# First four chunks of a gated recurrence taken whole instead of in halves, in a kernel that also runs an MLP

## The chip, the cores and the metric

The kernel runs on one core of a Trainium2 chip. The metric is the device time of one execution in microseconds (us). The engines are TensorE (PE, the matrix unit), VectorE (DVE), ScalarE (ACT), GpSimd (POOL) and SyncE (SP, which issues the DMAs here). Each engine works through its own list of instructions in order and waits on semaphores for the others.

## The reference

A gated linear recurrence over 768 steps, for 4 batches of 8 heads with 48 channels, feeds a two-layer MLP with a Mish-like gate.

```
f = 1 / (1 + exp(-f_logit))
for t in range(S):
    state = f[t] * state + outer(k[t], v[t])      # per batch and head, 48 x 48
    y[t] = q[t] @ state
x = y as (3072 tokens, 384)
h = x @ w_in                                       # (3072, 2048)
g = h * tanh(log1p(exp(h)))
out = g @ w_out                                    # (3072, 384)
```

## The kernel before

**The recurrence.** It is cut into 24 chunks of 128 steps: chunks 0 to 3 are the first of the four batches, chunks 4 to 7 the second of each, and so on. A chunk holds 4 pairs of heads (`NP`), a head on 64 rows each. `load` fetches the chunk's gate logits (`l`), keys and queries (`kq`) and values (`v`). `prep` forms the running sum of the log gates (on PE with a triangular matrix for chunks 0 to 3, by a scan on DVE later), then multiplies keys by its exponential (`inv`, on POOL for chunks 1 to 7) and queries by the inverse (on DVE, L373). `attn0` multiplies keys by queries (the scores), DVE masks them to the causal part into `a`. `attn1` transposes the keys on PE and ACT copies them to `kt`. `attn2` multiplies keys by values (the update). `attn3` forms the outputs `y`, and `leave` rounds them on ACT (L751, the high part of `xt`), subtracts that on PE with the matrix `minus` (L754) and copies the rest on ACT (L756, the low part). A small DMA then moves some rows of `xt` (L763).

Before the change a chunk is worked in two halves of 64 steps (`CH`). Scores are 64x64 blocks within a half. The update of the first half gives `mid`, the state between the halves, copied by ACT for chunks 0 to 3 (L648); that of the second half added to it gives `tmp` (DVE, L655), and POOL multiplies it by the chunk's decay into `state` (L740). The outputs sum products of queries with `mid` (and with `state`, from chunk 4 on) and of values with the masked scores (L673, L686). Chunk 3 (`ALONE`) has 18 further products (`pads`, L712), with weights in two small tiles lent by `g` and `n`, that place the fourth pair's rows where the other chunks use the DMA.

**The MLP.** Tokens come in 6 groups of 512, the four chunks of a batch position each (`GC` = 4). A unit is a group and one of the 16 slices of 128 hidden columns. Its first product `moe_in` (L297, 9 matmuls into `h`) needs `xt` of all four chunks, so the first one needs chunks 0 to 3 done. `mish` follows (ACT L311 exp, DVE L312, ACT L308, L314 and L315, DVE L316 for `g`, ACT L317 for `gh`, DVE or POOL for `gl`), then the second product `moe_out` (L324, 9 matmuls into `o`). `h` has two buffers, so the third unit's first product waits for `g` of the first unit. The weights of a slice arrive packed (`raw`, 768 KB, two buffers) and are split into a high and a low part by `split_w`: ACT L429, DVE L431, L432 and L434, ACT L436 (`wh`), DVE L437 (`wl`). The buffer is free when DVE L434 has read it.

**The order.** All of this is a list of steps, and the table `ORDER` gives the place of each step in its engine's list; a cost table in class `Plan` predicts when each starts. The loop in `issue` puts products on a tile of zeros (`idle`, L417) into PE's list ahead of the first second product wherever the plan has a gap:

```
while at + 527.0 < self.start[i]:
    self.idle()
    at += 427.0 if at > 6500.0 else 853.0
```

Of the kernel before, what the change touches and what calls it, by code (L numbers as in the profile page):

```python
# [159 lines left out]
class Plan:  # L160
# [61 lines left out]
    def issue(self):  # L222
        at = self.FREE["pe"]
        for i in self.order():
            engine, cost, issue = self.steps[i][:3]
            if engine == "pe":

                if self.start[i] <= self.start[self.until]:
                    while at + 527.0 < self.start[i]:
                        self.idle()  # L230
                        at += 427.0 if at > 6500.0 else 853.0
# [23 lines left out]
def recurrence_moe_kernel(  # L255
# [73 lines left out]
    with tc.tile_pool(name="work", bufs=1) as pool, tc.tile_pool(  # L329
# [327 lines left out]
        def attn3(n):  # L657
# [57 lines left out]
            def outputs():  # L715
# [5 lines left out]
                if n == ALONE:  # L721
                    pads()
# [310 lines left out]
```

## Time and profile before

| | us |
|---|---|
| median of 3 runs | 484.88 (484.2 to 486.53) |
| profiled execution, time | 487.03 |
| profiled execution, span from first to last instruction | 485.2 |
| PE busy in the span | 472.3 (97%) |
| ACT busy | 389.5 (80%) |
| DVE busy | 301.9 (62%) |
| POOL busy | 133.5 (28%) |

The span is what the profile's views divide. The profiled execution took 487.03 us, 1.8 us more than its span and 2.2 us more than the median. A busy PE is not a PE at its peak: its clock and the overlap of small products are read separately.

### The profile page before, as it was taken

The page shows a single profiled execution, that of the slowest core. Times are in us where ns is not written, and L with a number is a line of the kernel's source. Part 1 is how long each engine was busy: PE and PEld are TensorE (multiplying, and loading weights), DVE is VectorE, ACT ScalarE, POOL GpSimd, SP SyncE. Part 2 cuts the span into 40 slices and gives each one's busy share as a digit, 9 for nine tenths or more (in the row PEclk, how much of TensorE's full clock was granted, in tenths as well). Part 3 has the DMA queues.
Part 4 walks back from the last instruction along what each step waited for, and adds up shares of the span by engine and source line. Part 5 has one row for each costly group of instructions (what it writes and reads, how often), then busy time and mean ns, then how long its engine had stood idle before and what let it go on. Part 6 is the DMA issues. An engine that isn't in the chain of part 4 may idle for free.

```text
span 485.2 us, 11761 instructions
## 1 busy us (share of the span) xinstructions
PE 472.3 (97%) x4810; PEld 386.9 (80%) x4810; DVE 301.9 (62%) x523; ACT 389.5 (80%) x722; POOL 133.5 (28%) x125
## 2 busy tenths in 40 slices
PE   8898999999999999999999999999999999999995
PEld 6675778888888888888888888888888888888884
DVE  5886999999967766756557555655745433432221
ACT  6988899999996877987877887896776686867671
POOL 4522101000333124232423223243223242332422
PEclk9998999999999999999999999999999999999999
DMA  8975284365532582263435033253262000100001
GB/s 299 398 223 179 104 296 117 142 202 184 183 128 64 153 266 64 73 180 87 136 92 177 1 99 88 75 156 92 84 164 68 22 12 0 38 30 1 0 0 70
DMA packets 56604, 57.57 MB, mean 119 GB/s; under 512 B 36320, under 2 KB 39776, under 8 KB 56544
## 3 DMA queue, kind: packets, MB, share of 16 engines
q1 hardware_dynamic: 56544, 56.77, 37.8%
q8 instruction: 38, 0.62, 0.5%
q14 instruction: 22, 0.18, 0.1%
HBM read 43.25 MB, written 10.49 MB: 111 GB/s over the span
## 4 chain that ended last, share of the span: by engine, by line
PE 92%; DMA 3%; ACT 2%; issue 1%; DVE 1%; SPq 0%; ACTq 0%
PE o L324 41%; PE h L297 40%; DMA raw<-ww 3%; PE at L686 3%; PE at L602 3%; PE at L673 2%; PE at L536 2%; PE at L568 0%; PE at L754 0%; PE o L417 0%; ACT wt L429 0%; DVE wt L432 0%; DVE wt L434 0%; ACT xt L751 0%; PE at L486 0%
## 5 line engine op out<-in xcount | busy, mean ns | idle before, releaser
L319 POOL TENSOR_TENSOR gl<-g,gh 128x512 fp32r<-128x512 f32 x80 | 105.5, 1323 | 283.8 <-ACT gh L317 267.3
L297 PE MATMUL h<-xt,wh 128*128 128x512 f32 x576 | 180.6, 395 | 0.0
L297 PEld LDWEIGHTS h<-xt,wh 128*128 128x128 f32 x576 | 107.1, 189 | 23.0 <-DVE g L316 0.3
L316 DVE SCALAR_TENSOR_TENSOR g<-n,half,h 128x512 f32<-128x512 f32 x96 | 71.5, 745 | 82.6 <-ACT n L315 65.4
L324 PE MATMUL o<-gh,wh 128*128 128x512 f32 x288 | 113.4, 394 | 0.0
L297 PE MATMUL h<-xt,wl 128*128 128x512 f32 x288 | 112.9, 392 | 0.0
L324 PE MATMUL o<-gh,wl 128*128 128x512 f32 x288 | 112.2, 390 | 0.0
L324 PE MATMUL o<-gl,wh 128*128 128x512 f32 x288 | 112.2, 390 | 0.0
L311 ACT ACTIVATE n<-h 128x512 f32<-128x512 f32 x96 | 56.9, 592 | 42.5 <-PE h L297 41.9
L312 DVE TENSOR_SCALAR n<-n 128x512 f32<-128x512 f32 x96 | 42.6, 444 | 53.2 <-ACT n L311 52.8
L308 ACT ACTIVATE n<-n 128x512 f32<-128x512 f32 x96 | 60.1, 627 | 15.1 <-DVE n L312 14.8
L314 ACT ACTIVATE n<-n,ones 128x512 f32<-128x512 f32 x96 | 69.1, 720 | 1.7
L317 ACT ACTIVATE gh<-g 128x512 fp32r<-128x512 f32 x96 | 59.7, 623 | 7.1 <-DVE g L316 6.8
L297 PEld LDWEIGHTS h<-xt,wl 128*128 128x128 f32 x288 | 54.4, 189 | 11.5
L324 PEld LDWEIGHTS o<-gh,wh 128*128 128x128 f32 x288 | 54.1, 188 | 11.6
L324 PEld LDWEIGHTS o<-gl,wh 128*128 128x128 f32 x288 | 54.1, 188 | 11.3
L324 PEld LDWEIGHTS o<-gh,wl 128*128 128x128 f32 x288 | 54.1, 188 | 10.8
L315 ACT ACTIVATE n<-n 128x512 f32<-128x512 f32 x96 | 60.3, 628 | 1.6
L491 DVE TENSOR_TENSOR_SCAN cum<-go,l 128x512 f32<-128x512 f32 x20 | 27.8, 1392 | 2.8 <-ACT l L482 1.3
L373 DVE TENSOR_TENSOR kq<-kq,at 128x512 f32<-128x512 f32 (+1 forms) x38 | 25.3, 669 | 5.7 <-ACT at L499 3.8
L758 DVE TENSOR_TENSOR xt<-at,xt 128x256 fp32r<-128x256 f32 x32 | 13.0, 420 | 15.3 <-ACT xt L751 14.7
L602 PE MATMUL at<-v,kt 64*64 64x48 f32 x672 | 20.5, 221 | 1.8 <-issue 1.7
(135 smaller groups left out, 477.5 us busy)
## 6 DMA issues: line engine op xcount, KB each, us to landing
raw<-ww SPq DMA_DIRECT2D x16, 768.0 KB, 5.2
kq<-kq SPq DMA_DIRECT2D x23, 512.0 KB, 4.5
v<-vn SPq DMA_DIRECT2D x23, 256.0 KB, 4.5
l<-fl SPq DMA_DIRECT2D x20, 256.0 KB, 4.1
out<-ob SPq DMA_DIRECT2D x18, 256.0 KB, 3.0
kd<-inv SPq DMA_DIRECT2D x64, 64.0 KB, 2.2
kt<-kd SPq DMA_DIRECT2D x16, 256.0 KB, 2.9
xt<-xt SPq DMA_DIRECT2D x23, 128.0 KB, 2.7
```

The source lines that it names most:

```text
L297: nc.tensor.matmul(h, w[:, j, a * P : (a + 1) * P], xt[:, :, a, x, :], start=(n == 0), stop=(n == 3 * NK - 1))
L308: ("act", T_ACT(GT), 0, lambda: nc.scalar.activation(n, n, AF.Square))
L311: ("act", T_ACT(GT, True), 0, lambda: nc.scalar.activation(n, h, AF.Exp)),
L312: ("dve", 70 + GT / 1.92, 1, lambda: nc.vector.tensor_scalar(n, n, U_CAP, 1.0, ALU.min, ALU.add)),
L314: ("act", T_ACT(GT, False, 1), 0, lambda: nc.scalar.activation(n, n, AF.Ln, bias=ones)),
L315: ("act", T_ACT(GT), 0, lambda: nc.scalar.activation(n, n, AF.Exp, scale=-1.0)),
L316: ("dve", 662, 0, lambda: nc.vector.scalar_tensor_tensor(g, n, half_, h, ALU.subtract, ALU.mult)),
L317: ("act", T_ACT(GT), 0, lambda: nc.scalar.activation(gh, g, AF.Copy)),
L319: ("pool", T_POOL(GT), 1, lambda: nc.gpsimd.tensor_tensor(gl, g, gh.bitcast(F32), ALU.subtract)),
L324: nc.tensor.matmul(o, w[:, j, m * P : (m + 1) * P], x, start=(first and i == 0), stop=(last and i == 2))
L491: add("dve", 2 * T_DVE(w) - 70, lambda s=s, cum=cum: nc.vector.tensor_tensor_scan(cum.rearrange("p a c -> p (a c)"), go[:, s].rearrange("p ...
L602: return nc.tensor.matmul(u[c][half(e), p, :], kt[half(c), p, half(e)], moving, start=start, stop=True, skip_group_check=True,)
```

## The change

Chunks 0 to 3 are worked whole. Their state ahead is zero, so nothing but their own steps counts. Scores become full 128x128 products (8 instead of 16 for a chunk), with the mask over 512 columns and the results in a `square` of twice the width. The update is 8 products over all 128 steps instead of 16, and DVE multiplies the result by the decay straight into `state` (ACT's copy of `mid`, DVE's `tmp` and POOL's step fall away for these chunks). Outputs are 8 products of values with the masked scores, 128 columns each, instead of 24; chunk 3 has 6 further ones instead of 18, with one lent tile instead of two. The tiles `a`, `mid` and `tmp` move into one tile `parts`, in which the squares lie for chunks 0 to 3, and two POOL memsets of `mid` are gone. A product on zeros has 512 columns where the planned gap is long enough. `ORDER` is another table throughout. Later chunks compute as before.

```diff
-                        self.idle()
-                        at += 427.0 if at > 6500.0 else 853.0
+                        two = 1 + (at > 6500.0 and at + 954.0 < self.start[i])
+                        self.idle(two)
+                        at += 427.0 * two if at > 6500.0 else 853.0
...
+            if n < GC:
+                sc = [x.rearrange("p (a c) -> p a c", a=NP) for x in b]
+                for s in range(0, NP, st):
+                    todo = range(s, s + st)
+                    add("pe", 215 * st + 100, lambda todo=todo: [
+                        nc.tensor.matmul(sc[e][:, p, :], k[half(e), p, :], q[half(e), p, :], start=True, stop=True,
+                                         skip_group_check=True) for p in todo for e in range(2)
+                    ], thirds(("k", place(n)), todo) + thirds(("q", place(n)), todo), keys)
+                for e in range(2):
+                    dst, to = square(n, e)
+                    add("dve", T_DVE(GT), lambda e=e, dst=dst: nc.vector.tensor_tensor(
+                        dst, sc[e], tri[:, None, :].broadcast_to([P, NP, C]), ALU.mult), [keys[e]], to)
+                return
...
+                            nc.tensor.matmul(u[0][half(e), p, :], kt[:, p, half(e)], moving, start=True, stop=True,
+                                             skip_group_check=True)
+
+                add("pe", 450, whole, [("kt", n % 2), ("v", place(n))], keys[:1])
+                decay = ends[:, n].broadcast_to([P, NP, D]).rearrange("x p (r m) -> x p r m", m=3)
+                add("dve", T_DVE(NP * D), lambda: nc.vector.tensor_tensor(
+                    spread(st), u[0].rearrange("x p (r m) -> x p r m", m=3), decay, ALU.mult),
+                    pairs(("end", n)) + keys[:1], [ks])
+                return
...
-            if n < B:
-                add("act", T_ACT(NP * D, True), lambda: nc.scalar.activation(real(mid), flat[0], AF.Copy),
-                    keys[:1], [mk])
...
+                                nc.tensor.matmul(
+                                    y[e][half(x), a, :], v[:, c0 : c0 + 64], squares[e][0][:, 2 * a + x, :],
+                                    start=(a == 0), stop=True, skip_group_check=True)
...
-            if n < NCH - B:
+            if GC <= n < NCH - B:
```

PE's list where chunk 3 has its scores and its update. Before (`ob` and `n` are the tiles lent to chunk 3's queries, keys and values), the last two rows of the scores, a product on zeros and the start of the update:

```order
L536 MATMUL at_122<-ob_117,ob_116 64x64 x2
L536 MATMUL at_123<-ob_117,ob_116 64x64 x2
L417 MATMUL o_129<-state_73 128x256
L602 MATMUL at_124<-n_106,kt_92 64x48 x2
L602 MATMUL at_123<-n_106,kt_92 64x48 x2
```

After, the last two rows of the scores to the end of chunk 3's outputs (L698) and further products (L705):

```order
L546 MATMUL at_115<-ob_110,ob_109 128x128
L546 MATMUL at_116<-ob_110,ob_109 128x128
L771 MATMUL o_120<-xt_96,minus 128x256
L635 MATMUL at_117<-n_99,kt_92 64x48 x8
L771 MATMUL o_121<-xt_96,minus 128x256
L421 MATMUL o_122<-state_73 128x512
L698 MATMUL at_115<-parts,n_99 64x128 x2
L698 MATMUL at_116<-parts,n_99 64x128 x2
L705 MATMUL at_115<-parts,g_100 64x128 x4
L705 MATMUL at_116<-parts,g_100 64x128 x2
L421 MATMUL o_122<-state_73 128x512
```

The transposes of chunk 4's keys, which stood ahead of chunk 3's outputs, stand behind them now, and products on zeros have moved. Between the first four of them and the first `moe_in`, PE's list had six products on zeros of 256 columns; it has two of 256 and three of 512 now.

DVE's list from the end of slice 1's split (L434 before, L440 after) to chunk 3's masks. Before (`h` holds chunk 2's scores, `at` those of chunk 3):

```order
L434 SCALAR_TENSOR_TENSOR wt_121<-raw_119,wt_121 128x768
L480 TENSOR_SCALAR l_80<-l_80 128x512
L480 TENSOR_SCALAR l_81<-l_81 128x512
L549 TENSOR_TENSOR a_95<-h_125,causal 128x256
L549 TENSOR_TENSOR a_96<-h_126,causal 128x256
L437 TENSOR_TENSOR wl<-wt_120,wh 128x768
L491 SCALAR_TENSOR_TENSOR cum_90<-go_89,l_80 128x512
L655 TENSOR_TENSOR tmp_101<-at_123,mid_99 128x64x3
L373 TENSOR_TENSOR ob_117<-ob_117,at_122 128x512
L437 TENSOR_TENSOR wl<-wt_121,wh 128x768
L549 TENSOR_TENSOR a_98<-at_123,causal 128x256
L549 TENSOR_TENSOR a_97<-at_122,causal 128x256
```

After:

```order
L440 SCALAR_TENSOR_TENSOR wt_114<-raw_112,wt_114 128x768
L486 TENSOR_SCALAR l_80<-l_80 128x512
L443 TENSOR_TENSOR wl<-wt_113,wh 128x768
L551 TENSOR_TENSOR parts<-h_119,tri 128x512
L551 TENSOR_TENSOR parts<-h_118,tri 128x512
L640 TENSOR_TENSOR state<-at_117,ends 128x64x3
L380 TENSOR_TENSOR ob_110<-ob_110,at_115 128x512
L486 TENSOR_SCALAR l_82<-l_82 128x512
L497 SCALAR_TENSOR_TENSOR cum_90<-go_89,l_80 128x512
L443 TENSOR_TENSOR wl<-wt_114,wh 128x768
L551 TENSOR_TENSOR parts<-at_116,tri 128x512
L551 TENSOR_TENSOR parts<-at_115,tri 128x512
```

The masks are twice as wide, `wl` of slice 0 stands ahead of chunk 2's masks, and the state of chunk 2 has taken the place of `tmp`.

SP's list from the third slice's weights to the sixth's. Before (`raw_118` at the end is slice 4, `kq_84` and `v_87` belong to chunk 5, `v_86` to chunk 4, `kq_85` to chunk 6):

```order
L427 DMA raw_119<-ww 128x1536
L449 DMA l_80<-fl 128x512
L763 DMA xt_103<-xt_103 32x4x256
L454 DMA kq_84<-kq 128x1024
L763 DMA xt_103<-xt_103 32x4x256
L455 DMA v_87<-vn 128x512
L455 DMA v_86<-vn 128x512
L427 DMA raw_118<-ww 128x1536
L454 DMA kq_85<-kq 128x1024
L427 DMA raw_119<-ww 128x1536
```

After (`raw_111` is slice 4, the second `raw_112` slice 5):

```order
L433 DMA raw_112<-ww 128x1536
L780 DMA xt_96<-xt_96 32x4x256 x2
L455 DMA l_80<-fl 128x512
L780 DMA xt_96<-xt_96 32x4x256
L461 DMA v_86<-vn 128x512
L433 DMA raw_111<-ww 128x1536
L460 DMA kq_84<-kq 128x1024
L460 DMA kq_85<-kq 128x1024
L433 DMA raw_112<-ww 128x1536
L461 DMA v_87<-vn 128x512
```

Slice 4's weights stand ahead of the keys and queries of chunk 5 now, and the values of chunk 5 behind slice 5's weights.

## Rows read from the trace of the kernel before

**Rows 1.** The page's part 1: busy us (share of the span) xinstructions.

```profile
span 485.2 us, 11761 instructions
PE 472.3 (97%) x4810; PEld 386.9 (80%) x4810; DVE 301.9 (62%) x523; ACT 389.5 (80%) x722; POOL 133.5 (28%) x125
```

**Rows 2.** Stretches: length, busy PE, PEld, DVE, ACT, POOL, granted clock, DMA share, GB/s.

```profile
40.00:45.00 5.00, 2.80 (x10) 2.12 (x10) 3.71 (x6) 4.77 (x11) 0.00 (x0) 0.85 0.28 102
45.00:50.00 5.00, 5.00 (x122) 3.65 (x120) 4.19 (x10) 4.70 (x9) 1.45 (x2) 0.81 0.46 157
...
80.00:100.00 20.00, 20.00 (x149) 16.40 (x148) 19.91 (x33) 19.57 (x35) 0.00 (x0) 1.00 0.48 140
```

**Rows 3.** Timeline of PE, 19 to 43 us: start, us, engine, line, out<-in, [idle <-releaser].

```profile
19.77 1.05 PE L486 MATMUL at<-tri,g 128*128 128x128 f32 x8
20.75 0.68 PE L602 MATMUL at<-v,kt 64*64 64x48 f32 x31
23.14 0.20 PE L602 MATMUL at<-v,kt 64*64 64x48 f32 x1 [1.72 <-issue]
...
23.90 0.46 PE L673 MATMUL o<-kq,mid 64*64 64x64 f32 x16
...
25.08 0.66 PE L568 MATMUL at<-ident,ob 128*128 128x128 f32 x4
25.66 0.69 PE L536 MATMUL at<-ob,ob 64*64 64x64 f32 x32
26.29 0.70 PE L417 MATMUL o<-state 128*128 128x256 f32 x2
26.92 0.68 PE L602 MATMUL at<-n,kt 64*64 64x48 f32 x32
27.53 0.50 PE L754 MATMUL o<-xt,minus 128*128 128x256 f32 x2
28.07 0.63 PE L568 MATMUL at<-ident,kq 128*128 128x128 f32 x4
28.63 0.46 PE L673 MATMUL at<-ob,mid 64*64 64x64 f32 x16
...
30.84 0.70 PE L417 MATMUL o<-state 128*128 128x256 f32 x2
...
32.15 0.93 PE L297 MATMUL h<-xt,wh 128*128 128x512 f32 x2
...
42.27 0.66 PE L754 MATMUL at<-xt,minus 128*128 128x256 f32 x2 [2.20 <-ACT xt L751]
```

**Rows 4.** Timeline of ACT, 35 to 42 us.

```profile
35.09 0.58 ACT L311 ACTIVATE n<-h 128x512 f32<-128x512 f32 x1
...
38.51 0.91 ACT L429 ACTIVATE wt<-raw 128x768 f32<-128x768 f32 x1 [2.22 <-DMA raw<-ww]
...
41.86 0.64 ACT L751 ACTIVATE xt<-at 128x256 fp32r<-128x256 f32 x2
```

**Rows 5.** Timeline of DVE, 18 to 31 us.

```profile
18.04 1.04 DVE L434 SCALAR_TENSOR_TENSOR wt<-raw,wt 128x768 int32<-128x768 int32 x1
...
23.48 0.36 DVE L655 TENSOR_TENSOR tmp<-at,mid 128x192 f32<-128x192 f32 x1 [0.48 <-PE at L602]
...
26.42 0.76 DVE L549 TENSOR_TENSOR a<-at,causal 128x256 f32<-128x256 f32 x2 [1.08 <-PE at L536]
...
29.92 0.96 DVE L434 SCALAR_TENSOR_TENSOR wt<-raw,wt 128x768 int32<-128x768 int32 x1
```

**Rows 6.** The chain that ended last: start us, us, what.

```profile
30.91 7.58 DMA raw<-ww
...
42.93 3.48 PE h L297 x9
...
52.31 2.06 PE h L297 x9
```

**Rows 7.** The weights' DMA issues up to 62 us, in the view of their line.

```profile
DMA to landing us min/median/max: 4.2/7.4/9.1
```

More of the change, by code (lines that the diff above doesn't have):

```diff
@@ L340, in recurrence_moe_kernel, with square @@
         kt_, inv_ = (ring(nm, 2, [P, NP, C]) for nm in ("kt", "inv"))
-        a_ = ring("a", 4, [P, NP, CH])
-        mid_, tmp_ = (ring(nm, 2, [P, NP, 64]) for nm in ("mid", "tmp"))
+        parts_ = pool.tile([P, 8, NP * 64], F32, tag="parts", name="parts")
+        a_, mid_, tmp_ = (
+            [parts_[:, i].rearrange("x (p c) -> x p c", p=NP) for i in r] for r in (range(4), range(4, 6), range(6, 8))
+        )
+        part_keys = [("a", 0, 0), ("a", 0, 1), ("a", 1, 0), ("a", 1, 1), ("mid", 0), ("mid", 1), ("tmp", 0), ("tmp", 1)]
+        def square(n, e):
+            i = 4 * (n % 2) + 2 * e
+            return parts_[:, i : i + 2].rearrange("x h (p c) -> x (h p) c", p=2), part_keys[i : i + 2]
         xt_ = ring("xt", 2, [P, GC, NP, 2, C], F32R)
@@ L387, in recurrence_moe_kernel @@
             nc.vector.memset(x, 0.0)
-        for x in [state] + mid_:
-            nc.gpsimd.memset(x, 0.0)
-        spare = [x[:, : NK * P].rearrange("x (s a c) -> x s a c", s=NK, a=2) for x in (g_[0], n_[0])]
-        loan = (("g", 0), ("n", 0))
-        for x, key in zip(spare, loan):
-            add("pool", PADS, lambda x=x: nc.gpsimd.memset(x, 0.0), (), [key])
+        nc.gpsimd.memset(state, 0.0)
+        spare, loan = g_[0][:, : NK * P].rearrange("x (s a c) -> x s a c", s=NK, a=2), ("g", 0)
+        add("pool", PADS, lambda: nc.gpsimd.memset(spare, 0.0), (), [loan])
         def fill(dst, src, reads, writes):
@@ L414, in banks, with idle @@
             return ring[-1]
-        def idle():
-            nc.tensor.matmul(zeros[:, : 2 * P], state0[:, 0:P], state0, start=True, stop=True)
+        def idle(two):
+            nc.tensor.matmul(
+                zeros[:, : 2 * P * two].rearrange("x (a c) -> x a c", a=two), state0[:, 0:P],
+                state0[:, None, :].broadcast_to([P, two, 2 * P]), start=True, stop=True)
         def split_w(j):
@@ L553, in reads @@
                 return thirds(("k", place(n)), range(s, s + st)) + thirds(("q", place(n)), range(s, s + st))
-            if n >= GC:
-                late[n] = score, lambda: scores(0), mask, reads(0), keys
-            else:
-                for s in range(0, NP, st):
-                    add("pe", 140 * st + 50, lambda s=s: scores(s), reads(s), keys)
-                mask()
+            late[n] = score, lambda: scores(0), mask, reads(0), keys
         def attn1(n):
@@ L611, in update, with whole @@
                             add_to(p, e, c)
+            if n < GC:
+                def whole():
+                    for p in range(NP):
+                        for e in range(2):
+                            c0 = (2 * p + e) * 64
+                            moving = v[:, c0 : c0 + 64].rearrange("x (r m) -> x r m", m=4)[:, :, 0:3]
+                            nc.tensor.matmul(u[0][half(e), p, :], kt[:, p, half(e)], moving, start=True, stop=True,
[6 more added lines that the diff above has]
+                return
             if join:
@@ L639, in attn2 @@
                 mask()
-            elif n >= GC:
+            else:
                 _, scores, mask, reads, writes = late[n]
@@ L644, in attn2 @@
                 mask()
-            else:
-                add("pe", 640, update, [("kt", n % 2), ("v", place(n))], keys[: 2 - last])
-            if n < B:
-                add("act", T_ACT(NP * D, True), lambda: nc.scalar.activation(real(mid), flat[0], AF.Copy),
-                    keys[:1], [mk])
-                if n == ALONE:
-                    fill(spare[1][half(1)], mid[half(1), 2:NP], [mk], [loan[1]])
-            else:
-                add("dve", T_DVE(NP * D), lambda: nc.vector.tensor_tensor(real(mid), real(st), flat[0], ALU.add), keys[:1] + [ks], [mk])
+            add("dve", T_DVE(NP * D), lambda: nc.vector.tensor_tensor(real(mid), real(st), flat[0], ALU.add), keys[:1] + [ks], [mk])
             if not last:
@@ L659, in attn3 @@
             q, v = kq_[i][1], v_[i]
-            first, batch = n < B, n % B
+            batch = n % B
             mid, tmp, a_x = mid_[n % 2], tmp_[n % 2], a_[2 * (n % 2) :]
@@ L664, in attn3, with whole @@
             y = [x[:, 0 : 2 * C].rearrange("p (a c) -> p a c", a=2) for x in b]
+            if n < GC:
+                squares = [square(n, e) for e in range(2)]
+                if n == ALONE:
+                    fill(spare, v.rearrange("x (p e c) -> x p e c", p=NP, e=2)[:, 2:NP, 1], [("v", place(n))], [loan])
+                def whole():
+                    for a in range(2):
+                        for e in range(2):
+                            for x in range(2):
+                                c0 = (2 * (2 * a + x) + e) * 64
+                                nc.tensor.matmul(
+                                    y[e][half(x), a, :], v[:, c0 : c0 + 64], squares[e][0][:, 2 * a + x, :],
+                                    start=(a == 0), stop=True, skip_group_check=True)
+                    if n == ALONE:
+                        for s in range(NK):
+                            e, a = divmod(s, 2)
+                            for x in range(2):
+                                nc.tensor.matmul(
+                                    y[e][half(x), a, :], spare[:, s, x], squares[1][0][:, 2 + x, :],
+                                    start=False, stop=True, skip_group_check=True)
+                add("pe", 1650 if n == ALONE else 950, whole,
+                    [("v", i)] + squares[0][1] + squares[1][1] + [loan] * (n == ALONE), keys)
+                leave(n, y, keys, [])
+                return
             def inter(opens=True):
@@ L671, in inter @@
                             for e in range(2):
-                                if c or not first:
-                                    ran.append(nc.tensor.matmul(
-                                        y[e][half(x), a, half(c)], x_[half(e), 2 * a + x, :], q[half(e), 2 * a + x, half(c)],
-                                        start=(opens and a == 0 and c == first), stop=False, skip_group_check=True,
-                                    ))
+                                ran.append(nc.tensor.matmul(
+                                    y[e][half(x), a, half(c)], x_[half(e), 2 * a + x, :], q[half(e), 2 * a + x, half(c)],
+                                    start=(opens and a == 0 and c == 0), stop=False, skip_group_check=True,
+                                ))
                 return ran[0]
@@ L690, in intra @@
                 return one
-            def pads():
-                vp, mp = spare
-                for turn in (1, 0):
-                    todo = [[], []]
-                    for s in range(NK):
-                        e, a = divmod(s, 2)
-                        for x in range(2):
-                            for c in range(2):
-                                if (c ^ e) == turn:
-                                    todo[c].append((e, x, a, c, vp[half(c), s, x], a_x[1][half(c), 2 + x, :]))
-                            if (1 ^ e) == turn:
-                                todo[1].append((e, x, a, 1, mp[half(1), s, x], q[half(1), 2 + x, half(1)]))
-                    if not turn:
-                        stay_behind(one)
-                    for i in range(max(len(t) for t in todo)):
-                        for t in todo:
-                            if i < len(t):
-                                e, x, a, c, w, moving = t[i]
-                                one = nc.tensor.matmul(
-                                    y[e][half(x), a, half(c)], w, moving, start=False, stop=True, skip_group_check=True)
             def outputs():
@@ L720, in outputs @@
                 intra(1, 64)
-                if n == ALONE:
-                    pads()
-            if n == ALONE:
-                fill(spare[0], v.rearrange("x (p e c) -> x p e c", p=NP, e=2)[:, 2:NP, 1], [("v", place(n))], [loan[0]])
             qreads = thirds(("q", i)) + [("st", batch), ("mid", n % 2), ("v", i), ("a", n % 2, 0), ("a", n % 2, 1)]
@@ L730, in attn3 @@
             else:
-                if n == ALONE:
-                    qreads += loan
-                add("pe", 1850 if n == ALONE else 900 if first else 1150, outputs, qreads, keys)
+                add("pe", 1410, outputs, qreads, keys)
                 leave(n, y, keys, [])
```

207 rows, old and new, of the table ORDER are left out of this document.

## Prediction

> **What bounds the kernel now.** I read the busy times first [rows 1]: PE is busy for 472.3 of 485.2 us, so only time in which PE waits, runs zeros or runs slowly can be won, 13 us and what a lower clock hides. The stretches say where it is not. From 80 to 100 us PE is busy throughout at full clock, and DVE (19.91 of 20) and ACT (19.57) are as full as PE [rows 2]. From 40 to 45 us PE is busy for 2.80 of 5 us, and the granted clock is 0.85 there and 0.81 in the next stretch [rows 2].
>
> So two places matter. The first is the lead-in, all that runs before the first `moe_in` at 32.15 us [rows 3]; from there on PE's list holds the same products before and after. The second is the gap: PE waits 2.20 us at 42.27 for ACT's first rounding of chunk 4 [rows 3]. ACT is late because its list put the split of slice 4 ahead of it, and that sat 2.22 us for `raw` [rows 4], issued at 30.91 and landed 7.58 us later [rows 6]. After the gap the nine products of the third `moe_in` take 3.48 us, where nine at full clock take 2.06 [rows 6]: 1.42 us for the clock, in the stretches in which it was granted at 0.85 and 0.81, between its levels of 1.2 and 2.4 GHz. The gap costs 2.20 + 1.42 = 3.6 us. A hole of 1.72 us at 23.14 [rows 3], which the profile gives to no wait, lies in the lead-in too.
>
> Time after = time before, less what the first `moe_in` comes earlier, less what the gap shrinks, plus new waits. The sum is made in the span, 485.2 us; the profiled execution's own time was 487.03, the median 484.88. I take the difference off the median.
>
> **Small products.** An f32 product is two passes. Eight passes of 128 columns take 20.75 - 19.77 = 0.98 us, 0.122 each [rows 3]. A pass of 64 columns alone would then take 0.061, but 32 of them, each on a quarter of the array, take 26.29 - 25.66 = 0.63 us, 0.020 each [rows 3]: 3.1 of four overlap. The new products use half of the array each, in pairs. Nothing before runs in that shape; it overlaps between not at all and 2, and from 3.1 of 4 I take 1.55.
> - Scores of a chunk: 16 passes of 128 columns, 1.96 us alone, 1.26 at 1.55, 0.98 at 2; 0.63 before. They cost 0.6 more.
> - Outputs: 16 passes, likewise 1.26; before 25.08 - 23.90 = 1.18 [rows 3]. No change.
> - Chunk 3's outputs with its further products: 28 passes, 3.4 alone, 2.2 at 1.55, 1.7 at 2; before 30.84 - 28.63 = 2.21 [rows 3]. I take 1.9, between the last two.
> - Update: 16 passes of 48 columns (0.046 each), 0.73 alone, 0.47 at 1.55; before 26.92 to 27.53, 0.61 [rows 3]. At most 0.1 either way.
>
> In the Trainium skill, TensorE: Matmul & The Clock Gate, "Measured speedup vs the span model", products on distinct tiles of the array run side by side at about 4 ns a tile. The 64-column row agrees in kind (3.1 of 4). By that rule the 28 passes take 1.7 us and the forecast would be 481.4 instead of 481.6.
>
> **Zeros.** A product of 256 columns stands at 26.29 and the next step at 26.92: 0.63 us [rows 3]. One of 512 columns lies between 0.63 and 1.26; I take 0.9. Before, six of 256 are 3.8 us; after, two of 256 and three of 512 are 3.2 to 5.0, on the path only where PE would not wait anyway.
>
> **The lead-in.** Two chains meet at chunk 3's outputs.
> DVE first. From L434 at 18.04 to chunk 3's masks at 26.42 are 8.38 us, of which DVE waited 0.48 for the late pass of the hole and 1.08 for the scores [rows 5]; 6.82 are work. The order shows the same work there after, with chunk 2's masks twice as wide. Two masks of 256 columns take 0.76 [rows 5]; twice the width adds between 0 and 0.76, and I take 0.6. If slice 1's split ends when it did (its weights stand at the same place behind the same bytes), chunk 3's masks start at 18.04 + 6.82 + 0.6 = 25.5 and end 1.3 later, at 26.8; before 27.18. So DVE gives 0.4.
> PE: without the hole chunk 2's outputs can start when their masks are there, and its scores cost 0.6 more, still ahead of DVE's 26.8. PE waits for the masks, then runs the outputs (1.9, to 28.8), zeros (0.9, under which ACT rounds), the subtraction (0.4), the transposes of chunk 4 (28.63 - 28.07 = 0.56 [rows 3]) and a short product on zeros (0.5): the first `moe_in` at 31.0. Before, the same stretch was bound by PE itself: update, subtraction and transposes stood between scores and outputs. The gain is 32.15 - 31.0 = 1.1 us. If the hole comes back at 1.72, PE is late again and about 0.3 is left; if zeros and masks are at their lower ends, the first `moe_in` stands at 29.7 and 2.4 are won.
> ACT's copy of `mid`, POOL's `state` step and DVE's `tmp` fall away or are replaced size for size; PE's list, not they, stood behind the 32.15, so I cost them at nothing. Their cover is the wait for the masks; without it ACT's copies would be worth some tenths.
>
> **The gap.** `raw` of slice 4 can be issued when DVE has split slice 2. Before, that ended at 29.92 + 0.96 [rows 5], 3.7 us after chunk 3's masks. After, those operations follow the masks without the wait for an update between: L437, state, L438, L440, about 2.5 us: issue at 29.3 instead of 30.91. SP's order now has only `v` of chunk 4 shortly ahead and the 1 MB for chunks 5 and 6 behind. Its landing takes between 4.2 and 7.58 us [rows 6, 7]: 33.5 to 36.9. ACT came to it at 38.51 - 2.22 = 36.29, 4.1 us behind the first `moe_in`; after, 31.0 + 4.1 = 35.1. The wait is 0 to 1.8 instead of 2.22, and I take 0.6. The hole of 1.72 at 23.14 was not followed by a lower clock in its stretch, the 2.20 at 42.27 was; at 0.6 I count no clock loss. Of 3.6 us, 0.6 stay.
> The order also moves `v` of chunk 5 behind `raw` of slice 5. That `raw` waits for slice 3's split, which follows the masks as before: issued about 35.7. Chunk 5's update stands right behind the third `moe_in`, about 10.3 us behind the first one if the gap is gone (42.93 + 3.48 - 32.15 = 14.3 [rows 3, 6], less 3.6, and the transposes already out of the way): 41.4. If `raw` and `v` together take 5.5 to 7.5 us, they land at 41.2 to 43.2: a new wait of 0 to 1.8, and I take 0.8. PE's whole list stands behind that update. So 2.2 of the 3.6 are won.
>
> Sum: 1.1 + 2.2 = 3.3 us; 484.88 - 3.3 = **481.6** (span 481.9).
>
> **The rivals.**
> *The gap stays.* The lead-in is shorter, but `raw` lands late all the same, as its transfer takes 7.4 us in the median [rows 7]: ACT then waits 36.7 - 35.1 = 1.6, the values of chunk 5 come at 43 or later, PE stands still twice and the clock falls. Only the lead-in is left: 483.8, or 484.9 where the DMA paces all. For it: what ACT waited for was a transfer. Against it: 1 MB moved behind it.
> *DVE sets the pace behind the lead-in.* It is 19.91 of 20 us busy from 80 to 100 [rows 2], its masks come only 0.4 earlier and are 0.6 wider in each of four chunks. If nothing else counts, 0.4 to 2 us are won: 482.9 to 484.5. Against it: DVE has idle time before (1.29 of 5 us from 40 to 45 [rows 2]), which goes with the gap.
> *The half-array products don't overlap.* Chunk 3's outputs take 3.4, its scores 0.7 more: the first `moe_in` at 32.8; with the gap's 2.2 the time is 483.3. The change then does the opposite of its words in the lead-in.
> *Slower: the values of chunk 5.* If `raw` of slice 5 takes the longest landing seen, 9.1 us [rows 7], and the 256 KB behind it 1.5 more, chunk 5's update waits from 41.4 to 46.3, and the clock falls behind it: 4.9 + 1.4 = 6.3, against 3.6 before, less 1.1 of the lead-in: 486.5. It decides from a landing at about 44.7 on (3.3 + 1.4 = 3.6 + 1.1).
>
> **How the numbers follow.** Forecast 0.50 (479.5 to 483.0), the gap stays 0.20, DVE paces 0.13, no overlap 0.07, the values late 0.10. Half a per cent is 2.4 us, about what a measurement of this kernel tells from no change. Faster means below 482.5: nine tenths of the forecast and the lucky ends of the others, 0.52; slower, above 487.3, only the worst of the late values and of products that don't overlap with a gap that stays, 0.07; the rest, 0.41, is the same. The range of 478.8 to 486.2 takes in the lead-in's 2.4 with the whole gap (484.9 - 2.4 - 3.6 = 478.9) below, and most of the late values above.
>
> **What would show it.** In the profile after: the first L297 near 31.0; chunk 3's outputs (L698 and L705) with 28 passes in 1.7 to 2.2 us (3.4: no overlap); L551 at 1.2 to 1.5 us for a chunk; ACT's wait on `raw` ahead of L435 near 35 below 1.8; the third `moe_in` at 2.0 to 2.1 us and no stretch of lower clock from 40 to 50. I am wrong if PE's wait has moved to the update of chunk 5 (L617 waiting for a DMA), if the first `moe_in` is no earlier, or if PE waits for DVE between 50 and 100 us.

## The result, and the profile after

The changed kernel takes 487.69 us (median of 12 executions, 484.19 to 489.37), the kernel before beside it 484.70 (12, 482.96 to 488.86): ratio 1.0052, 95% interval 1.0029 to 1.0076. It is a little slower. 481.6 was forecast; the range of 478.8 to 486.2 does not hold it, and faster had the larger chance. The profiled execution took 488.83 us.

The page's part 1 of the changed kernel, against [rows 1]:

```profile
span 487.1 us, 11187 instructions
PE 474.9 (98%) x4528; PEld 388.3 (80%) x4528; DVE 306.2 (63%) x523; ACT 387.7 (80%) x718; POOL 130.1 (27%) x117
```

Stretches, columns as in [rows 2]:

```profile
40.00:45.00 5.00, 5.00 (x122) 3.81 (x124) 4.84 (x11) 4.97 (x11) 1.40 (x2) 1.00 0.50 196
45.00:50.00 5.00, 4.78 (x65) 3.49 (x58) 5.00 (x8) 4.76 (x11) 1.04 (x1) 1.00 0.58 213
...
163.00:166.00 3.00, 1.04 (x19) 0.54 (x19) 1.17 (x2) 1.59 (x4) 1.95 (x2) 1.00 0.87 278
166.00:171.00 5.00, 4.99 (x119) 4.43 (x120) 1.27 (x3) 1.50 (x3) 1.29 (x1) 0.66 0.61 178
```

The gap at 42 us is gone, PE busy and the clock at full. A new one of the same kind stands 120 us later: PE is busy for 1.04 of 3 us, and then the clock is granted at 0.66.

PE's timeline in the lead-in, to be laid beside [rows 3]:

```profile
21.67 1.12 PE L421 MATMUL o<-state 128*128 128x512 f32 x2
22.73 1.09 PE L698 MATMUL o<-parts,v 128*64 128x128 f32 x16
23.75 0.66 PE L583 MATMUL at<-ident,ob 128*128 128x128 f32 x4
...
27.52 1.09 PE L698 MATMUL at<-parts,n 128*64 128x128 f32 x16
28.45 0.82 PE L705 MATMUL at<-parts,g 128*64 128x128 f32 x12
29.20 1.13 PE L421 MATMUL o<-state 128*128 128x512 f32 x2
...
31.04 0.59 PE L297 MATMUL h<-xt,wh 128*128 128x512 f32 x1
```

A chunk's outputs take 23.75 - 22.73 = 1.02 us, chunk 3's 28 passes 29.20 - 27.52 = 1.68, a zero product of 512 columns 0.74 to 1.06. PE has no hole from 21.67 us on, and the first `moe_in` starts at 31.04; 31.0 was forecast. ACT takes slice 4 without the 2.22 us wait of [rows 4]:

```profile
34.56 0.90 ACT L435 ACTIVATE wt<-raw 128x768 f32<-128x768 f32 x1
```

The waits of PE in the whole span (us in total, times, longest):

```profile
PE at L617 <- DMA kt<-kd: 2.0, 1, 2.0
PE o L421 <- DVE state L392: 1.2, 1, 1.2
PE at L583 <- DVE kq L380: 1.1, 1, 1.1
PE h L297 <- DVE g L316: 0.9, 2, 0.6
```

The first is chunk 11's. From chunk 8 on DVE transposes a chunk's keys, four DMAs write them to DRAM (`kd`) and a fifth reads them back (`kt`). PE's timeline there:

```profile
163.58 0.46 PE L733 MATMUL at<-parts,v 64*64 64x64 f32 x16
166.01 0.22 PE L617 MATMUL at<-v,kt 64*64 64x48 f32 x1 [1.97 <-DMA kt<-kd]
...
168.51 1.22 PE L297 MATMUL h<-xt,wh 128*128 128x512 f32 x2
```

SP's timeline shows what stands ahead of the read:

```profile
155.59 2.57 SPq L592 DMA_DIRECT2D kd<-inv  x4
158.25 0.56 SPq L455 DMA_DIRECT2D l<-fl  x1
158.91 0.39 SPq L857 DMA_DIRECT2D out<-ob  x1
159.85 0.32 SPq L594 DMA_DIRECT2D kt<-kd  x1
160.26 0.59 SPq L780 DMA_DIRECT2D xt<-xt  x1
```

and the same place in the kernel before:

```profile
158.46 2.57 SPq L577 DMA_DIRECT2D kd<-inv  x4
161.08 0.62 SPq L840 DMA_DIRECT2D out<-ob  x1
163.96 0.33 SPq L579 DMA_DIRECT2D kt<-kd  x1
164.54 0.32 SPq L815 DMA_DIRECT2D ob<-half  x1
```

The view of the read's line, at this issue alone, gives its landing, after and before:

```profile
DMA to landing us min/median/max: 6.0/6.0/6.0
```

```profile
DMA to landing us min/median/max: 2.6/2.6/2.6
```

Before, `kt` landed at 163.96 + 2.6 = 166.6, and PE's list came to it 0.7 us later, without a wait:

```profile
167.25 0.21 PE L602 MATMUL at<-v,kt 64*64 64x48 f32 x1
```

After, PE comes 3.2 us earlier (at 164.04), the read is issued 4.1 us earlier and lands at 165.9. From the issue of the first key write PE comes 8.8 us later before (158.46 to 167.25) and 8.5 after (155.59 to 164.04); to the landing of `kt` it takes 8.1 us before and 10.3 after.

Where each kernel's profile won and lost, from the starts of the products into h of units 5, 24, 29, 54 and 90 (us; the difference to the first profile of before in brackets, and alone in the three columns behind it):

| kernel | unit 5 starts | 5 to 24 | 24 to 29 | 29 to 54 | span |
|---|---|---|---|---|---|
| before | 63.93 | (82.33 us) | (24.91 us) | (119.68 us) | 485.2 |
| before, again (h1) | 64.00 (+0.1) | +0.1 | 0.0 | +1.2 | 486.5 |
| f2 wide zeros alone | 61.00 (-2.9) | 0.0 | 0.0 | +0.7 | 483.0 |
| e3 old start, new order | 60.66 (-3.3) | +0.5 | +1.1 | +1.1 | 484.9 |
| after | 59.46 (-4.5) | +1.1 | +3.7 | +0.7 | 487.1 |
| after, again (f1) | 59.16 (-4.8) | +1.4 | +2.2 | +0.8 | 485.6 |
| e4 narrow zeros | 62.23 (-1.7) | 0.0 | +0.5 | +0.7 | 485.6 |
| e1 `kt` first | 59.52 (-4.4) | 0.0 | +1.2 | +0.8 | 483.8 |
| g1 shifted code | 60.35 (-3.6) | 0.0 | +0.7 | +1.1 | 484.2 |
| g2 both | 60.73 (-3.2) | 0.0 | 0.0 | +1.9 | 484.7 |
| e2 new start, old order | 60.17 (-3.8) | 0.0 | 0.0 | 0.0 | 481.6 |
| f4 e2, narrow zeros | 60.12 (-3.8) | +0.6 | 0.0 | 0.0 | 482.2 |
| f3 old order from unit 24 | 59.63 (-4.3) | +0.1 | 0.0 | 0.0 | 481.7 |

From unit 54 to 90 all agree within 0.11 us. The changed kernel's line closes: -4.46 + 1.08 + 3.73 + 0.72 + 0.05, and 0.77 behind unit 90, is the 1.9 by which its span is longer. Each row is one execution. The row of e4 is the slowest of its twelve: its first `moe_in` is late, and its clock was at half from 9.9 us, behind a wait of 2.0 us:

```profile
10.00:13.40 3.40, 3.40 (x35) 2.80 (x34) 1.75 (x4) 2.58 (x5) 1.27 (x1) 0.51 1.02 417
```

The waits for `g` begin with a transfer. In the changed kernel the weights of slice 7 landed 6.1 us after their issue, and ACT, then DVE, then PE (0.61 us at 65.41) waited:

```profile
61.27 0.90 ACT L435 ACTIVATE wt<-raw 128x768 f32<-128x768 f32 x1 [1.01 <-DMA raw<-ww]
```

The same weights took 5.9 us in f1, and 4.2 to 4.6 in the other eleven profiles.

### The profile page after: what moved, and what is told of

It is laid out like the page before. It is cut to its first block, busy times and chain, and to the rows that moved or that the text cites. A ratio compares the mean times of both kernels' runs of the same rounds, so it can differ in the third digit from the quotient of the medians.

```text
span 487.1 us, 11187 instructions
## 1 busy us (share of the span) xinstructions
PE 474.9 (98%) x4528; PEld 388.3 (80%) x4528; DVE 306.2 (63%) x523; ACT 387.7 (80%) x718; POOL 130.1 (27%) x117
## 4 chain that ended last, share of the span: by engine, by line
PE 82%; DMA 7%; DVE 6%; ACT 3%; SPq 1%; issue 1%; DVEq 0%; ACTq 0%
PE o L324 36%; PE h L297 36%; PE at L733 2%; DMA raw<-ww 2%; PE at L617 2%; DMA kq<-kq 2%; PE at L720 2%; PE at L556 1%; DMA kt<-kd 1%; DMA v<-vn 1%; DVE g L316 1%; DVE wt L440 1%; DVE cum L497 1%; ACT wt L435 1%; DVE kq L380 1%
## 5 line engine op out<-in xcount | busy, mean ns | idle before, releaser
L312 DVE TENSOR_SCALAR n<-n 128x512 f32<-128x512 f32 x96 | 46.6, 486 | 57.2 <-ACT n L311 56.8
L497 DVE TENSOR_TENSOR_SCAN cum<-go,l 128x512 f32<-128x512 f32 x20 | 26.6, 1329 | 1.6 <-ACT at L508 1.6
L768 ACT ACTIVATE xt<-at 128x256 fp32r<-128x256 f32 (+1 forms) x44 | 15.6, 374 | 9.4 <-PE at L733 8.9
```

The lines of the kernel that those rows point to most:

```text
L312: ("dve", 70 + GT / 1.92, 1, lambda: nc.vector.tensor_scalar(n, n, U_CAP, 1.0, ALU.min, ALU.add)),
L497: add("dve", 2 * T_DVE(w) - 70, lambda s=s, cum=cum: nc.vector.tensor_tensor_scan(cum.rearrange("p a c -> p (a c)"), go[:, s].rearrange("p ...
```

## The experiments

Theory T: the first chunks win what was forecast, and the new order of steps behind them loses it, above all at chunk 11's `kt`. Rival P: a PE that is 3 to 4 us early meets late transfers there in any order. Rival Z: the wide zeros do it.

A ratio is to the kernel before beside the same runs, which differs from chip to chip: its median was 486.80 us (32 executions) beside e1 to e4, 485.00 (35) beside f1 to f4 and 485.70 (23) beside g1 and g2. The changed kernel itself was measured again beside f2 to f4 alone.

**e1, `kt` first.** SP's list of the changed kernel:

```diff
 L592 DMA kd_124<-inv_94 512x1x32 x4
-L455 DMA l_81<-fl 128x512
-L857 DMA out<-ob_110 128x512
 L594 DMA kt_92<-kd_124 128x512
+L455 DMA l_81<-fl 128x512
+L857 DMA out<-ob_110 128x512
```

> The changed kernel with one edit: on SP, the load of l of chunk 14 and one store of out (256 KB each), which stand between the four key writes (kd) of chunk 11 and the read of its kt, are issued behind that read. In the changed kernel's profile the read landed 6.03 us after its issue at 159.85 us, PE waited 1.97 us for it at 166 us and its clock was then at half for 3.41 us. Theory T (the loss is in the new order of steps behind the first chunks, above all these two transfers ahead of kt): kt lands in at most 3.5 us, PE doesn't wait there, no half clock near 166 us, and the profiled time falls by 3.0 to 3.7 us, to about 485; the ratio to the kernel before is 0.996 to 1.000. Rival P (a PE that is 3.4 us ahead meets a late transfer or a late engine there in any order): the wait stays or another over 1 us comes within 20 us of it, and the ratio stays at 1.004 to 1.008.

Measured: 485.13 us, ratio 0.9975 (0.9946 to 1.0003). The wait was halved, not ended:

```profile
PE at L617 <- DMA kt<-kd: 1.0, 1, 1.0
```

```profile
DMA to landing us min/median/max: 5.2/5.2/5.2
```

The time came out as T says, but `kt` took 5.2 us with nothing of those two ahead of it. They are only a part of the cause.

**e2, the new start with the old order; e3, the old start with the new order.** In e2 the table is the changed one up to unit 5 and the old one, renumbered, behind it (the edit is written here as a rule, the kernel holds the table); e3 is the mirror image.

```diff
-ORDER = NEW
+ORDER = NEW[:320] + [i - 10 for i in OLD if i >= 124 and i - 10 not in NEW[:320]]
```

> The changed kernel with its own order of steps up to the product into h of unit 5 (59 us), and behind it, on every engine, the steps in the relative order of the kernel before. Theory T: the 4.46 us that the changed kernel is ahead at unit 5 stay but for at most 1.5 us, no wait of PE over 1 us behind 60 us; the time is 480 to 482.5, ratio 0.990 to 0.995. Rival P (PE ahead meets late transfers whatever the order): 3 us or more of the lead are lost again, time 484 to 488, ratio 0.998 to 1.006.

> The kernel before with its own first chunks, its own zero products and its own order up to the product into h of unit 5, and behind it, on every engine, the steps in the changed kernel's relative order. Theory T: no gain ahead and the changed kernel's losses behind (1.1 us at the waits for g, 3.7 us at kt of chunk 11, about 1 us later): 488 to 491, ratio 1.007 to 1.013. Rival P: PE is as late as before and nothing is met, time 484 to 486, ratio 0.998 to 1.003.

Measured: e2 483.47 us, ratio 0.9927 (0.9900 to 0.9954), e3 486.66, ratio 1.0021 (0.9991 to 1.0051). e2 (9 executions) keeps 3.7 of its 3.8 us to unit 90, and its profile has no wait of PE behind 60 us. P falls: in the old order the keys of chunk 11 start earlier with PE (first write at 154.74, before 158.46), and though the read took 4.2 us, `kt` landed 0.4 us ahead of its use. What e2 does have is the wait for the values of chunk 5 that was forecast:

```profile
42.75 0.46 PE L617 MATMUL at<-v,kt 64*64 64x48 f32 x17 [0.92 <-DMA v<-vn]
```

e3 loses 2.8 us between units 5 and 90 in its profile, as T says, but its ratio is where P had it, and shows no loss clear of noise: it started 3.3 us ahead of the first profile of before, with the same first steps. That gap was not always there (h1, below). So T's price for the new order alone is not borne out by the times.

**e4, narrow zeros; f2, wide zeros alone.**

```diff
-                        two = 1 + (at > 6500.0 and at + 954.0 < self.start[i])
+                        two = 1
```

f2 puts the changed `idle` and the line marked - into the kernel before.

> The changed kernel with the products on zeros 256 columns wide everywhere, as in the kernel before. Theories T and P: no difference to the changed kernel but run to run, ratio 1.003 to 1.008, first product into h within 0.5 us of 31.04 us. Rival Z (the wide zero products do harm, or are what holds the clock at full through 50 us): over 1.5 us to either side, with a stretch at half clock ahead of 60 us if it is slower.

> The kernel before with the second part of the change alone: products on zeros of 512 columns where its own planned gap ahead of the first product into h allows it. Theory T: ratio 0.998 to 1.002. Rival Z (the wide zero products cost or bring time by the clock or by the first product's start): outside 0.995 to 1.005.

Measured: e4 485.03 us, ratio 0.9955 (0.9929 to 0.9980), which neither T nor P expected; f2 486.53, 1.0022 (0.9990 to 1.0055), no clear difference. In e4 `kt` of chunk 11 landed after 2.6 us. It has 12 TensorE instructions more, all ahead of unit 0. That led to theory I: instructions arrive in packets of their own DMA queue, and where these fall depends on that count. The stretch at half clock that Z asked for is there in e4's profile (at 9.9 us), but its time is lower, not higher.

**f1, the changed kernel again.** Not a line differs.

> The changed kernel once more, not a line different, on the chip and beside the kernels of this call. Theory T (its later order loses part of what the first units win): it is slower than the kernels of this call that have the order of before behind unit 5 by 1.5 to 4 us; its second profile shows waits for g, kt and v behind 60 us again, of other lengths than 0.9, 2.0 and 0. If the 2.0 us wait and the half clock at 166 us are there again, they belong to the order; if not, they were one outcome of several, and the ratio is expected at 0.996 to 1.004.

Measured: 487.60 us, ratio 1.0042 (1.0009 to 1.0075). The slowdown repeats. So do the landing of 6.0 us and the wait of 2.0, so they are not one execution's; the half clock is not in both: here the clock stays at full behind the same wait.

```profile
166.00:170.00 4.00, 4.00 (x122) 3.55 (x123) 0.99 (x3) 1.50 (x3) 1.09 (x1) 1.00 0.69 198
```

**f3, the old order from unit 24 on; f4, e2 with narrow zeros.** f3 is e2's edit with 650 for 320; f4 is e2 with e4's line.

> The changed kernel with its own order of steps up to about 138 us (unit 23), and behind it the relative order of the kernel before on every engine. Theory T with its loss at chunks 11 and 12 (kt at 160, v at 164 to 190 us): the lead over the kernel before at unit 25 is kept to the end within 0.8 us, no wait for kt over 0.5 us; ratio 0.991 to 0.996, about 1 us above the kernel with the order of before from unit 5 on. If the loss is spread over the whole later order, half of it stays: ratio 0.996 to 1.000.

> The changed kernel with the order of before behind unit 5, and products on zeros of 256 columns. Theory T: as with the wide ones (ratio 0.990 to 0.995, 483 to 484 us). Rival Z: the first product into h comes 1 to 2 us later, as in the one profile of the changed kernel with narrow zeros (33.29 against 31.04 us), and with it the end: ratio 0.994 to 0.999.

Measured: f3 483.81 us, 0.9975 (0.9946 to 1.0003); f4 483.68, 0.9963 (0.9935 to 0.9992). Beside f1 they are 3.8 and 3.9 us faster, the nearest comparison with the changed kernel; f1 and f3 have the same list up to unit 23. f3 keeps 4.2 of 4.3 us to unit 90 in its profile; its ratio is weaker than expected. Not all of the loss sits behind 138 us: up to unit 24 the two profiles of the changed kernel lost 1.1 and 1.4 us, and f3, e1, e4, g1 and g2, with the same order there, at most 0.1. Those waits for `g` come with the late weights of slice 7, and what makes these late is open. Narrow zeros make no clear difference here (f4 against e2): what e4 won is not the zeros' time. Of P a little stays: f4 lost 0.6 us in the old order, by a wait of 0.51 at 86.5 us for chunk 8's `kt`.

**g1, shifted code; g2, shifted code and `kt` first.** The packets of the queue that brings instructions (read from the packet records; start and length in us, the 16 KB packet nearest to chunk 11's keys, and the issue and landing of the read of `kt`):

```
after  packet 162.0 2.42   kt 159.8 -> 165.9
f1     packet 162.4 1.96   kt 159.9 -> 165.9
e1     packet 160.1 2.30   kt 158.8 -> 164.0
e4     packet 160.4 1.45   kt 163.3 -> 165.9   (last kd took 3.9)
g1     packet 157.8 1.31   kt 160.8 -> 164.2   (two of kd took 3.7 and 3.4)
g2     packet 158.2 1.35   kt 161.3 -> 163.9   (two of kd took 3.8 and 3.4)
```

```diff
-        at = self.FREE["pe"]
+        at = self.FREE["pe"] + 4 * 853.0
+        order = self.order()
+        for _ in range(44):
+            self.pad()
+        none = state0.bitcast(mybir.dt.bfloat16)
+        plan.pad = lambda: nc.tensor.matmul(zeros[:, 0:16], none[:, 0:P], none[:, 0:16], start=True, stop=True)
```

> The changed kernel with TensorE's instruction stream shifted: the four products on zeros that open the kernel (1.2 to 4.8 us) are replaced by 44 small ones (bfloat16 zeros, 16 columns), about 70 instructions more ahead of everything else; orders and all later work as in the changed kernel. In its two profiles a 16 KB packet of the queue that brings instructions (started at 162.0 and 162.4 us, 2.42 and 1.96 us long) lies inside the flight of kt of chunk 11 (issued at 159.8 and 159.9, landed after 6.0); in the kernel with narrow zeros, 12 instructions more, it came at 160.4, ahead of the read, which then landed after 2.6. Theory I (the instruction packet holds one DMA engine and with it the whole read): the packet comes 5 to 9 us earlier, ahead of the key writes at 155 us, kt lands in at most 4.2 us, PE's wait for it is at most 0.6 us instead of 2.0; median 484 to 486, ratio 0.996 to 1.001. Theory T alone (the transfers ahead of kt on SP make it late): kt lands after 5 to 6 us, the wait is 1.5 to 2.2 us, ratio 1.003 to 1.007.

> Both edits: the shifted instruction stream, and on SP the load of l of chunk 14 and one store of out behind the read of kt of chunk 11. If the packet and the two transfers each add to kt's landing: it lands in at most 3.2 us, PE has no wait for it, and of the lead at unit 25 at most 0.3 us is lost by unit 29; ratio 0.993 to 0.999. If the two transfers matter and the packet not: as the kernel with kt first alone (landing 5.2 us, wait 1.0 us, ratio 0.9975). If the packet matters and the transfers not: as the kernel with the shifted stream alone.

Measured: g1 485.81 us, 1.0003 (0.9978 to 1.0029); g2 484.91, 0.9987 (0.9968 to 1.0007). In g1 the packet came 4.2 us earlier, less than meant, and fell on the key writes; the read then took 3.3 us, and PE waited 0.5 for it. In g2 it took 2.7, and PE did not wait:

```profile
DMA to landing us min/median/max: 3.3/3.3/3.3
```

```profile
DMA to landing us min/median/max: 2.7/2.7/2.7
```

The read alone overstates the packet, since in g1 the key writes took longer instead. From the issue of the first key write to the landing of `kt`, chunk 11 took 10.3 us in both profiles of the changed kernel, 9.4 in e1, 9.2 in e3, 8.8 in g1, 8.6 in e4 and 8.1 in g2; with the old order there (before, h1, f2, e2, f3, f4) 7.2 to 8.5. PE came 8.8 us behind that first issue in all six profiles of the old order, and 8.3 to 8.5 behind it in the seven of the new one. So the new order leaves 0.3 us less room, and PE waits where the keys took longer than the room.

Both edits count: putting the two transfers behind the read takes off 0.8 us (10.3 to 9.4) or 0.6 (8.8 to 8.1), shifting the code 1.5 (10.3 to 8.8) or 1.3 (9.4 to 8.1). That the shift works through the packet is argued. In e2, f3 and f4 a packet ran inside the read too (from 160.2, 159.3 and 159.9 us, for 1.31, 0.92 and 1.03), and the read landed after 4.2, 3.4 and 3.0. Of the 208 reads of `kt` in the 13 profiles, the 31 with such a packet in flight took 2.5 to 6.0 us, median 3.6, the others 2.5 to 5.0, median 2.8. A long packet may also be a sign of busy DMA engines and not its cause.

g2 still lost 1.9 us between units 29 and 54, more than any other. Of that, 0.9 is a wait for the keys of chunk 13, whose read took 5.0 us with no packet in flight:

```profile
PE at L620 <- DMA kt<-kd: 0.9, 1, 0.9
```

Its expectation counts the lead from unit 25, which stands at another place in the new order; from unit 24 to unit 29 g2 lost nothing.

**h1, the kernel before again.**

> The kernel before, unchanged, for a second profile. In its first one (487.03 us, 2.15 above its median) PE stood still for 2.20 us at 42.27 us and the clock was at half for 3.41 us from 43.5; two kernels that share its first 59 us of order reached the product into h of unit 5 at 60.7 us or earlier, with no half clock, where it came at 63.93. If the half clock belongs to that one execution, this profile has none ahead of 60 us, unit 5 starts between 60 and 62 us, and of the 3.6 us put down to the gap at most 1.5 are there to be won in most executions. If it belongs to the kernel, there is a stretch at half clock between 40 and 50 us and unit 5 starts at 63 to 64.5 us.

Measured: one execution, 488.32 us. The gap is there again, as in [rows 3], with the clock at half from 43.4 us:

```profile
42.30 0.66 PE L754 MATMUL at<-xt,minus 128*128 128x256 f32 x2 [2.31 <-ACT xt L751]
```

So it is not one execution's mishap. e3, with the same first steps, has 0.5 us of it, and f2, with wide zeros in them, none:

```profile
40.67 0.66 PE L757 MATMUL at<-xt,minus 128*128 128x256 f32 x2
```

In f2 slice 4's `raw` landed 5.2 us after its issue, 5.9 in e3, where it took 7.6 and 7.3 in the two profiles of before. Of the 35 executions of before beside f2, 12 have a mean granted clock of at most 0.996 and take 485.89 to 489.18 us; the other 23 take 482.72 to 485.83. Both profiles of before (clock 0.995 and 0.994) are of the first sort. Beside e1 to e4, 14 of 32 have such a clock, beside g1 and g2 7 of 23, and there the times of the two sorts overlap (up to 487.28 us at a clock of 0.997 or more). That most executions run without the gap is argued from the clock, since only profiles show it.

h1 also lost 1.2 us against the first profile behind unit 29, at the keys of chunk 12:

```profile
183.03 0.22 PE L602 MATMUL at<-v,kt 64*64 64x48 f32 x1 [0.99 <-DMA kt<-kd]
```

## Why the prediction was wrong

**The lead-in: right.** First `moe_in` at 31.04 (31.0 forecast), chunk 3's outputs 1.68 (1.9), scores 1.09 a chunk (1.26), zeros of 512 columns 0.74 to 1.06 (0.9), no hole. In the other eight profiles with the new start the first `moe_in` stands at 30.4 to 33.3. The forecast's "to 28.8" is 28.7 by its own terms; 31.0 follows from them all the same.

**The gap: its mechanism right, its price not.** In the profile after, ACT has no wait for slice 4 (0.6 forecast), the update of chunk 5 none for `v` (0.8 forecast), and no clock is lost before 60 us: 3.4 of the 3.6 us are won by unit 5, more than the 2.2 forecast. The wait for `v` is there in five of the other eight profiles with the new start: 0.63 us in e1, 0.92 in e2, 0.48 in e4, 0.20 in f1, 0.83 in g1. So its 0.8 was sound, and its absence in one profile luck. The first step that failed is "I take the difference off the median": the gap was priced from an execution of 487.03 us, and the median, 484.88, is of executions of which most, by their clock, don't have it. Against the starts without it (f2, e3) the changed kernel is only 1.2 to 1.8 us ahead at unit 5.

**Nothing behind the first products: wrong, and this gave the sign.** "From there on PE's list holds the same products before and after" was true of which products, and I took it to hold of their times; the sum's "plus new waits" has none behind chunk 5. `ORDER` is another table on every engine to the end. From unit 5 to unit 90 the changed kernel loses 5.6 us in its first profile and 4.4 in the second, where e2 loses 0.1. Of the 4.4, 2.2 fall at chunk 11's `kt` (a wait of 1.96), 1.4 at the waits for `g` (1.1 of waits), 0.8 between units 29 and 54. In the first profile 3.7 us fall at `kt`, with the same wait and half clock for 3.41 us from 166.9.

All seven profiles with the new order lose 0.7 us or more between units 29 and 54, five of them 0.7 to 1.1 without a wait of PE there. Four of the six with the old order lose nothing; h1 and f2 lose 1.2 and 0.7 by waits for chunk 12's `kt` (0.99 and 0.46). The 0.8 behind unit 90 lies behind the last product: from its end to the last instruction are 6.0 us after and 5.3 before. f3 has it too, e2 and e3 don't; its cause is open.

**The rivals.** "DVE sets the pace" named the waits for `g`, 0.9 to 1.1 us behind unit 5 in the two profiles, though they begin with late weights. "Slower: the values of chunk 5" had the right mechanism, a transfer late behind others and the clock behind the wait, at the wrong chunk. Poor overlap of half-array products is refuted by the 1.68 us.

Together: 1.2 to 1.8 us won at the start against an execution without the gap, f1's 4.4 lost up to unit 90: 2.6 to 3.2 slower, 0.8 more with the end, 0.7 to 1.2 less against an execution that waits at chunk 12 as f2 and h1 do. The medians say 2.6 to 3.0. The sum is of single executions, so the agreement is loose.

What wins is the change with the old order behind unit 5: e2 at 0.9927 of the kernel before, and f4, the same with narrow zeros, at 0.9963, where the changed kernel beside it stood at 1.0042.

## What to carry to other kernels

When a change comes with a new order, compare the order over the whole program and look for the transfers that just made it: `kt` of chunk 11 landed at 166.6 and was used at 167.25, so 0.7 us was all that stood between this kernel and a stall, and 0.25 in h1. Measure the room of such a chain, from its first issue to its use, against what it takes: 8.8 us against 7.2 to 8.5 held, 8.5 against 8.6 to 10.3 did not. Price a stall from more than one execution before taking it off a median. A read behind a write through DRAM is better issued ahead of bulk transfers that nobody waits for: here that was worth 0.6 to 0.8 us.

## What the hardware showed unexpectedly

Instructions arrive by DMA beside the data. One 16 KB packet of their queue ran for 2.42 us at 162.0 us while `kt` was in flight; in a stretch of 2.6 us that one packet is 5.8% of the time of 16 engines:

```profile
q8 instruction: 1, 0.02, 5.8%
```

The same kind of packet took 0.88 us at 126.7. The Trainium skill, Runtime: NRT & Kernel Launch, "Instruction fetch mechanics", says that engines refill their instruction memory in 16 KiB blocks and that a boundary costs "one DMA tail-bump, mostly hidden". The size agrees with the trace. Whether the cost stayed hidden here is not shown for certain: with the code shifted by some 70 instructions, chunk 11's keys took 1.3 to 1.5 us less from first write to landing, and PE waited 0.45 us instead of 1.97; that the packet did it is argued.

The same wait of 2.0 us of PE was followed by 3.41 us at half clock in one profile and by full clock in the other. Products on half of the array overlapped fully in pairs: 28 passes in 1.68 us, 0.060 each, where one of 128 columns takes 0.122.
